# Two score tiles converted in one VectorE instruction, against single-tile conversions in two separate PSUM tiles, with a re-set planner

## The chip, the cores and the metric

The kernel runs on one core of a Trainium2 chip. The metric is the device time of one execution in microseconds (us). Five engines work side by side, each in the order in which its own instructions stand in the program: TensorE (PE in the profile: matmuls; PEld: its weight loads), VectorE (DVE), ScalarE (ACT), GpSimd (POOL) and SyncE (SP, which here issues nearly all DMAs). Engines wait for each other through semaphores.

## The reference

Two attention blocks share the input `x` (2048 rows, 512 columns, 32 heads of width 16) and are mixed by a gate:

```python
g = sigmoid((x * gate_w).sum(-1))
a = A(x): q,k,v = x @ wqkv; softmax(q k^T / 4) v over all 2048 keys; @ wo
b = B(x): the same, but each query sees 8 keys: itself and those 2,4,...,14 rows before; @ wo
out = g * a + (1 - g) * b
```

A needs 32 x 2048 x 2048 exponentials. In tiles of 128 keys by 512 queries of one head these are 2048 score tiles, called units below.

## The kernel before, in words

**Periods.** The 32 heads are 8 groups of 4, and the queries 4 blocks of 512. A pair of group and block is a period: 32 periods with 16 key tiles x 4 heads = 64 units each.

**Two ways for a unit.** Most units go through ScalarE: PE writes scores into a ring of two PSUM tiles `ring` of 3 and 2 units in turn (`fillA`), ACT computes the exponential of 3 or 2 units at once into `pT` (1536 or 1024 elements per partition), and PE multiplies with V into `acc` (`pvA`, groups of four matmuls in four column strips). Some go through VectorE, four at a time (a quad, made by `make_quad`): PE writes one unit into one of two PSUM banks named `m` (`fillD`), DVE turns the scores into an integer that read as bfloat16 approximates the exponential (`conv`, writes `dt`), DVE makes two shifted copies for a better approximation (`term`, 2048 elements per partition each), and PE adds all three, weighted, into `acc` (`pvD`, three groups of four matmuls). When a period's units are all in, DVE transposes `acc` to `accT`, takes the reciprocal `rden`, POOL scales into `ott`, DVE transposes back.

**The same two banks serve everything else on PE**: projections of K, Q, V (evacuated by DVE to `kr`, `qr`, `vp_all`), B's projections (`bw` times `xT`, evacuated to `kvs`), the sum over B's window (`ident` times `pv`), the output projections (`woarr`, `bwo`, evacuated to `osb`). In the kernel before, both banks are one tile, allocated once, and a user gets a half of it:

```python
mm_t = ps.tile([128, 2, QW], FP32, tag="mm", bufs=1, name="mm_ps")
def misc_ps(hold, shape):
    v = mm_t[:, hold.k, 0:math.prod(shape[1:])]
```

**B's local attention** runs tile by tile (16 tiles of 128 rows, `b_tile`) on POOL: products `prod`, sums `lg`, softmax with help of DVE and ACT, products `pv`, then PE sums over the window.

**The order is planned at build time.** `Sched` is a list scheduler written in Python: each operation has an engine, a planned duration, dependencies, resources (`acq`, `rel`), and a due time. Step by step it takes the operation that can start soonest, the earliest due first among near ones, and emits its instructions; this fixes the order on each engine. The waits between engines are not the planner's: the tile framework sets semaphores from the tiles that the emitted instructions read and write. The planner counts the two `m` banks as two resources.

**Names that the change touches.** `STREAM` and `LEAST` (L59, L60) steer zero-weight passes: `warm` asks what share of the last 3413 ns PE streamed and puts in passes of four matmuls with weights of zero, for free if the share is under `STREAM`, and at the cost of a delay (up to 450 ns) if it is under `LEAST`. `MARGIN` adds slack to planned hand-overs between engines. `join` (in `make_quad`) puts two units of a quad together where both banks are free at the planned time: two fills, then one `conv` over 1024 elements. `start_quad` and `d_source` decide when a quad is begun (`LATE`, `QUAD`, `UNIT`, at most 3 at once). `hooks` sets, at the begin of each period, the due times of projections and starts B's tiles (`b_next`, one for each 1.7 periods).

Of the kernel before, what the change touches and what calls it, by code (L numbers as in the profile page):

```python
# [23 lines left out]
QW = 512  # L24
# [12 lines left out]
def _mean_log_ratio():  # L37
    n = 4096
    acc = 0.0
    for k in range(n):  # L40
        y = 128.0 * k / n
        s = 0.0
        for o, w in zip(OFFS, WTS):
# [10 lines left out]
SEM = 50.0  # L54
PASS = 216.0
SWITCH = 100.0
OVERDUE = 500.0
KB_NS = 6.5
XFER = 1900.0  # L59

MARGIN = {("POOL", "DVE"): 1500.0, ("POOL", "PE"): 1500.0, ("DVE", "PE"): 200.0, ("PE", "DVE"): 60.0,
          ("ACT", "DVE"): 1000.0, ("DVE", "POOL"): 800.0, ("SP", "PE"): 1000.0, ("DVE", "SP"): 300.0, ("SP", "POOL"): 1500.0, ("POOL", "ACT"): 1000.0}
WINDOW = 3413.0
STREAM = 0.48
LEAST = 0.42
FAST = 682.0


# [7 lines left out]
class Op:  # L76
    __slots__ = ("eng", "fn", "dur", "mms", "deps", "due", "allow", "acq", "rel", "lat", "start", "fin", "vis",
                 "name", "not_before", "after", "begun", "prompt", "zeros", "closing",
                 "lock", "gap", "kb", "ahead")

    def __init__(self, eng, fn, dur=0.0, mms=None, deps=(), due=None, allow=1000.0, acq=(), rel=(), lat=0.0,
                 name="", not_before=0.0, after=None, begun=(), prompt=False,
                 lock=False, kb=0.0):
        self.ahead = None
        self.kb = kb
        self.eng, self.fn, self.dur, self.mms = eng, fn, dur, mms
        self.deps = [d for d in deps if d is not None]
        self.due, self.allow, self.acq, self.rel, self.lat = due, allow, list(acq), list(rel), lat
        self.begun = [d for d in begun if d is not None]
        self.start = self.fin = self.vis = None  # L90
        self.prompt = prompt
        self.zeros = 0
        self.closing = False
        self.lock = lock
        self.gap = 30.0
        self.name, self.not_before, self.after = name, not_before, after
# [26 lines left out]
class Sched:  # L123
# [82 lines left out]

    def commit(self, op, ready):
        e = op.eng
        if op.ahead is not None:
            op.ahead(max(ready, self.t[e]))  # L210
        for h in op.acq:
            h.k = self.slots[h.res].take()
        if e == "PE":
# [107 lines left out]
    def pick_pe(self, near, cands):  # L321
        urgent = [c for c in cands if c[0].name == "fillA"]
        first = min(max(self.t["PE"], c[1]) for c in near)
        same = [c for c in near if c[0].mms[0][0] == self.pe_mode]
        tight = [c for c in near if c[0].mms[0][0] != self.pe_mode and c[2] < first + 600.0 and c[0].name != "fillA"]
        order = (same + [c for c in near if c not in same]) if same and not tight else near
        if not urgent:
            return order[0]
        u = urgent[0]
        limit = u[2]  # L330
        for c in order:
            if c[0] is u[0]:
                return c
            _, _, st = self.pe_run(c[0].mms, c[1])
            first, _, _ = self.pe_run(u[0].mms, u[1], st)
            alone, _, _ = self.pe_run(u[0].mms, u[1])
            if first <= max(limit, alone + 30.0):
                return c
        return u
# [3 lines left out]
def kernel(  # L343
# [58 lines left out]
    def mm(out, lhsT, rhs, start, stop, **kw):  # L402
        return T.matmul(out, lhsT=lhsT, rhs=rhs, start=start, stop=stop, **kw)
# [16 lines left out]
    for k in range(KEPT, KEPT + 28):  # L420
        S_.slots["keep"].free[k] = INF


    mm_t = ps.tile([128, 2, QW], FP32, tag="mm", bufs=1, name="mm_ps")

    def misc_ps(hold, shape):
        v = mm_t[:, hold.k, 0:math.prod(shape[1:])]
        if len(shape) > 2:
            v = v.rearrange("p (a b) -> p a b", a=shape[1])
        return v  # L430

    def sb(hold, shape, dtype, name):
        return work.tile(shape, dtype, name=name, tag=f"{hold.res}_{hold.k}", bufs=1)
# [795 lines left out]
    def pe_source(e):  # L1229
# [8 lines left out]
        if us and w < INF:  # L1238
# [3 lines left out]
            if r < INF and S_.slots["pTA" if n == 3 else "pTB"].when() < INF:  # L1242
# [3 lines left out]
                op = Op("PE", None, mms=[("r", u[2], 512) for u in us], name="fillA")  # L1246
                op.fn = lambda us=us, res=res, n=n, op=op: emit_fill(us, res, n, op)
                op.after = after_fill
                outl.append((op, r, act_idle - 480.0))

        if pv_wait:
            p = pv_wait[0][0]
# [13 lines left out]
            if whole or full:  # L1266
                a = acc_ready(p)
                if a is not None:
                    vs = [vp_ops[(u[1], 4 * periods[p][1] + u[2])].vis for u in batch]
                    if all(v is not None for v in vs):  # L1270
# [5 lines left out]
                        op.closing = npv[p] <= 8  # L1276
                        op.fn = lambda p=p, batch=batch, op=op: emit_pva(p, batch, op)
                        op.after = lambda o, p=p, batch=batch: after_pva(o, p, batch)
                        outl.append((op, r, batch[0][3] + (2000.0 if sum(used) < 5 else -2000.0)))

        for q in pvd_ready:
            a = acc_ready(q["p"])
# [10 lines left out]
            op.closing = npv[q["p"]] <= 8 and q["next"] == len(OFFS) - 1  # L1293
            op.fn = lambda q=q, op=op: emit_pvd(q, op)
            op.after = lambda o, q=q: after_pvd(o, q)
            outl.append((op, r, min(q["vis"] + 4000.0, q["late"])))
            break
        return outl

# [93 lines left out]
            pv_commit(q["p"], op)  # L1393


    LATE = 2000.0
    QUAD = 6000.0
    UNIT = 470.0
    quad_at = [0]
    quad_end = [None]  # L1400
    JOIN = 100.0

    def soon(o, late):
        if o.due is not None:
# [35 lines left out]
    def make_quad(p, t, late):  # L1440
# [4 lines left out]
        def term_tile():  # L1445
            q["terms"].append(sb(hq[len(q["terms"])], [128, 4, QW], U16, "dt"))
        aops, fops = [], []
        holds, both = [Hold("m") for _ in range(4)], set()

        def fill(j):  # L1450
            f_ = fops[j]
            for _ in range(f_.zeros):
                mm_ct(mm_t[:, 0 if j in both else holds[j].k, :], zw, ones_t[:], True, True)
            for j_ in ((j, j + 1) if j in both else (j,)):
                mm(mm_t[:, j_ - j if j in both else holds[j].k, :], kt_all[32 * j_:32 * j_ + 32, i, t * 128:(t + 1) * 128],
                   qt_tiles[periods[p]][32 * j_:32 * j_ + 32, :], True, True, tile_position=(32 * j_, 0))

        def conv(j):
            if j == 0:
                term_tile()  # L1460
            V.tensor_scalar(out=q["terms"][0][:, j:j + 2, :] if j in both else q["terms"][0][:, j, :],
                            in0=mm_t[:] if j in both else mm_t[:, holds[j].k, :], scalar1=EXP_MULT, scalar2=EXP_ADD,
                            op0=ALU.mult, op1=ALU.add)

        def join(j, at):

            f1, f2, a1, a2 = fops[j], fops[j + 1], aops[j], aops[j + 1]
            if S_.slots["m"].when(2) + (MARGIN["DVE", "PE"] if at > 25000.0 else 0.0) > at + JOIN:
                return
            both.add(j)  # L1470
            S_.pend["PE"].remove(f2)
            S_.pend["DVE"].remove(a2)
            f1.mms = f1.mms + f2.mms
            f1.acq += f2.acq
            a1.rel += a2.rel
            a1.dur = 1217.0

            def same(o, o2):
                o2.start, o2.fin, o2.vis = o.start, o.fin, o.vis
            f1.after = lambda o: same(o, f2)  # L1480
            a1.after = lambda o: same(o, a2)
        for j in range(4):
            f_ = S_.add(Op("PE", lambda j=j: fill(j), mms=[("r", j, 512)], deps=[qt_ops[periods[p]][0], kdep(p, t)],
                           begun=fops[-1:] or [quad_end[0]], allow=0.0,
                           acq=[holds[j]] + ([] if j else hq[:1]), name="fillD"))
            fops.append(f_)
            quad_end[0] = f_
            a_ = S_.add(Op("DVE", lambda j=j: conv(j), dur=683.0, deps=[f_] + aops[-1:], due=min(S_.now, late - 6000.0) + 300.0 * j - 5000.0,
                           rel=[holds[j]], name="conv"))
            aops.append(a_)  # L1490
            if j % 2 == 0:
                f_.ahead = lambda at, j=j: join(j, at)
        tops = []
        for k in range(1, len(OFFS)):
            def term(k=k):
                term_tile()
                V.tensor_scalar(out=q["terms"][k][:], in0=q["terms"][0][:], scalar1=float(OFFS[k]), scalar2=None, op0=ALU.add)
            tops.append(S_.add(Op("DVE", term, dur=FAST, lock=True, deps=aops + tops[-1:], acq=[hq[k]], due=min(S_.now + 7000.0 + 1500.0 * k, late - 4000.0 + 1000.0 * k), name="term")))

        def done(o):  # L1500
            d_busy[0] -= 1
# [3 lines left out]
        d_busy[0] += 1  # L1505

    def d_source(e):
        if e == "PE" and d_busy[0] < 3:
            if any(o.due is not None and o.due < S_.now and S_.est(o) is not None for o in S_.pend["PE"] if o.name != "fillD"):
                return []  # L1510
            dve = sum(o.dur for o in S_.pend["DVE"] if S_.est(o) is not None)
            if dve + max(0.0, S_.t["DVE"] - S_.now) < 3000.0 and S_.now > 22000.0:
                start_quad()
        return []

# [22 lines left out]
    def hooks(p):  # L1538
# [7 lines left out]
            g_jobs(now + 8000.0)  # L1546
        m = p // 8
        if p % 8 == 1 and m + 1 < NPR:
            k_due(m + 1, now + 0.3 * TPER, 4.2 * TPER)
            v_due(8 * m + 8, 8 * m + 16, now + 1.5 * TPER, 4.5 * TPER)  # L1550
        if p % 2 == 0 and p + 2 < NP:
            q_pair(periods[p + 2][0], periods[p + 2][1] // 2, now + 0.8 * TPER)
        if p == NP - 8:
            wo_jobs([o for i_ in range(NG) for o in kt_ops[i_]] + list(vp_ops.values()))
        while b_proj_next[0] < NT and b_proj_next[0] <= p + 1:
            b_proj(b_proj_next[0], now + (2000.0 if p > 2 else 22000.0))
            b_proj_next[0] += 1
        if len(b_proj_ops) == NT and all(o.start is not None for o in b_proj_ops):
            b_proj_ops.clear()
            for k in range(KEPT + 16, KEPT + 28):  # L1560
                S_.slots["keep"].give(k, now)
        while b_next[0] < NT and b_next[0] * 1.7 <= p:
            b_tile(b_next[0], now + (2000.0 if p > 2 else 22000.0))
            b_next[0] += 1

# [67 lines left out]
```

## Time and profile before

| | |
|---|---|
| three runs | 963.09, 963.73, 969.73 us; median 963.73 |
| profiled execution | 963.73 us, span 961.9 us, mean granted PE clock 0.888 |
| busy | PE 800.3, ACT 765.5, DVE 640.0, POOL 608.3 us |
| ACT, exponentials | 643 instructions for 1608 units, 758.1 us busy, 154.7 us idle just before them |
| DVE, conversions | 398 of 512 elements (684 ns), 21 of 1024 (1213 ns) |
| DVE, terms | 220 of 2048 elements, 859 ns |
| zero-weight matmuls | 728 into `acc` (128 of them open its 32 periods), 20 into the `m` banks, 24 into `ring` |

The span runs from the first to the last instruction of the core; the execution is 1.8 us longer. "Idle before" counts the time an engine stood still just ahead of an instruction, and the releaser is the instruction whose end let it go. Because a helper records every operation, all instructions carry one line number, so groups are told apart by tiles: `mm_ps` is the tile of the two `m` banks. A granted clock of 1.0 is PE at full speed and 0.5 at half; the trace has it in windows of 3.41 us.

### The profile page before, as it was taken

The numbers are of one execution on the slowest core, as the hardware profiler recorded it, in microseconds if no ns is written. First come the engines' busy times: TensorE is split into PE (matmuls) and PEld (weight loads), VectorE is DVE, ScalarE is ACT, GpSimd is POOL, SyncE is SP. The second block draws the span as 40 slices with busy tenths as digits, with TensorE's granted clock in tenths as the row PEclk, the third lists the DMA queues.
The fourth block names the chain that finished last, engine by engine and source line by source line (L and its number), as shares of the span: only waits on it lengthen the run. The fifth ranks groups of instructions, "written<-read, shape, count | busy, mean of one in ns | idle before, by whom it ended". The sixth has DMA issues, their size and how long they took to land.

```text
span 961.9 us, 25343 instructions
## 1 busy us (share of the span) xinstructions
PE 800.3 (83%) x10830; PEld 252.0 (26%) x10830; DVE 640.0 (67%) x1009; ACT 765.5 (80%) x665; POOL 608.3 (63%) x909
## 2 busy tenths in 40 slices
PE   6888887988888887888879888787799998898975
PEld 2232222322232232222213223232312132222221
DVE  4646766577846777577667695778767676665644
ACT  1977778897975997789778899888878798779880
POOL 1015867788236978598187897979765789862300
PEclk9988899997987999899779989999967599779797
DMA  9121022230202123021211212122121213110000
GB/s 220 46 95 66 29 83 79 78 116 26 80 19 89 45 90 117 22 91 50 79 61 46 72 46 84 45 73 88 37 72 45 72 51 88 47 61 30 12 7 28
DMA packets 66801, 62.09 MB, mean 65 GB/s; under 512 B 14848, under 2 KB 64128, under 8 KB 66688
## 3 DMA queue, kind: packets, MB, share of 16 engines
q1 hardware_dynamic: 65104, 60.28, 19.9%
q8 instruction: 84, 1.38, 0.6%
q10 hardware_dynamic: 1584, 0.20, 0.1%
q14 instruction: 29, 0.24, 0.1%
HBM read 43.91 MB, written 12.62 MB: 59 GB/s over the span
## 4 chain that ended last, share of the span: by engine, by line
PE 54%; DVE 32%; ACT 8%; issue 4%; DMA 0%; DVEq 0%; ACTq 0%
PE mm_ps L393 29%; DVE dt L393 22%; PE acc L393 15%; PE ring L393 9%; ACT pT L393 8%; DVE kvs L393 2%; DVE qr L393 1%; DVE kr L393 1%; DVE kt_all L393 1%; DVE vp_all L393 1%; DVE osb L393 1%; DVE accT L393 1%; DVE kmax_all L393 1%; PE warm L393 1%; DVE bw L393 1%
## 5 line engine op out<-in xcount | busy, mean ns | idle before, releaser
L393 ACT ACTIVATE pT<-ring 128x1536 bf16<-128x1536 f32 (+1 forms) x643 | 758.1, 1249 | 154.7 <-PE ring L393 132.5
L393 DVE TENSOR_SCALAR dt<-mm_ps 128x512 uint16<-128x512 f32 (+1 forms) x419 | 292.7, 710 | 178.4 <-PE mm_ps L393 135.3
L393 PE MATMUL ring<-qt,kt_all 32*128 32x512 bf16 x1608 | 306.6, 419 | 11.9 <-ACT pT L393 9.8
L393 PE MATMUL mm_ps<-qt,kt_all 32*128 32x512 bf16 x440 | 159.3, 424 | 78.7 <-DVE dt L393 57.7
L393 POOL TENSOR_TENSOR pv<-vsh,lg 128x256 bf16<-128x256 bf16 x256 | 175.0, 706 | 32.6 <-PE mm_ps L393 17.7
L393 POOL TENSOR_TENSOR prod<-ksh,qb 128x256 f32<-128x256 bf16 x256 | 180.9, 736 | 16.4 <-DMA ksh<-kv_scr 12.6
L393 DVE TENSOR_SCALAR dt<-dt 128x2048 uint16<-128x2048 uint16 x220 | 186.2, 859 | 1.9 <-PE acc L393 0.3
L393 POOL TENSOR_TENSOR prod<-prod 128x256 f32<-128x256 f32 (+1 forms) x256 | 183.6, 727 | 5.6
L393 PEld LDWEIGHTS <-kt_all 32*128 32x128 bf16 (+1 forms) x2304 | 88.2, 93 | 348.5 <-issue 335.1
L393 PE MATMUL acc<-pT,vp_all 128*17 128x512 bf16 x1608 | 143.3, 425 | 0.0
L393 POOL TENSOR_TENSOR ott<-accT,rden 128x256 bf16<-128x256 f32 x31 | 22.3, 721 | 139.8 <-DVE rden L393 139.8
L393 PE MATMUL acc<-dt,vd_all 128*17 128x512 bf16 x880 | 83.3, 416 | 0.0
L393 PE MATMUL acc<-ones_t,zw 128*32 128x512 bf16 x728 | 76.7, 473 | 3.1 <-DVE accT L393 2.6
L393 PE MATMUL mm_ps<-bw,xT 128*32 128x512 bf16 x768 | 61.8, 416 | 17.2 <-DVE dt L393 11.7
L393 PEld LDWEIGHTS <-vp_all 128*17 128x17 bf16 x2048 | 41.3, 91 | 95.1 <-issue 83.8
L393 POOL TENSOR_TENSOR lg<-lg,rr 128x256 f32<-128x256 f32 x16 | 10.7, 669 | 75.7 <-DVE rr L393 67.7
L393 PEld LDWEIGHTS <-xT 128*32 128x32 bf16 (+1 forms) x1920 | 38.4, 101 | 63.4 <-issue 57.3
L393 PE MATMUL acc<-dt,vp_all 128*17 128x512 bf16 x440 | 48.4, 429 | 0.0
L393 PE MATMUL mm_ps<-ident,pv 128*32 128x128 bf16 x2048 | 40.7, 222 | 6.4 <-DVE dt L393 5.6
L393 DVE CAST kvs<-mm_ps 128x512 bf16<-128x512 f32 x32 | 21.7, 683 | 25.8 <-PE mm_ps L393 21.9
L393 PEld LDWEIGHTS <-pv 128*32 128x32 bf16 x2048 | 32.3, 97 | 22.0 <-issue 18.3
L393 PEld LDWEIGHTS <-zw 128*32 128x32 bf16 x772 | 19.2, 102 | 70.6 <-issue 67.0
(82 smaller groups left out, 409.4 us busy)
## 6 DMA issues: line engine op xcount, KB each, us to landing
ksh<-kv_scr SPq DMA_DIRECT2D x16, 1024.0 KB
vsh<-kv_scr SPq DMA_DIRECT2D x16, 1024.0 KB
kv_scr<-kvs SPq DMA_DIRECT2D x16, 384.0 KB
q_scr<-qr SPq DMA_DIRECT2D x32, 128.0 KB
qt<-q_scr SPq DMA_DIRECT2D x31, 128.0 KB
qb<-kv_scr SPq DMA_DIRECT2D x16, 128.0 KB
out_dram<-osb SPq DMA_DIRECT2D x16, 128.0 KB
kt_all<-kr SPq DMA_DIRECT2D x112, 16.0 KB
```

What stands on the lines that cost most here:

```text
L393: return chain_on(key, f(*a, **k))
```

## The change

The conversion is always of one unit: `join` goes away, and with it the one tile over two banks. Each bank is a tile of its own (`m0_ps`, `m1_ps`), allocated anew for each user. Beside this, planner constants and due times are set anew. GpSimd's halved instructions and the zero-weight passes that may delay PE are in both kernels; of the passes only the two thresholds change.

```diff
-OVERDUE = 500.0
+OVERDUE = -500.0
-MARGIN = {("POOL", "DVE"): 1500.0, ...
+MARGIN = {("POOL", "DVE"): 1000.0, ...
-STREAM = 0.48
-LEAST = 0.42
+STREAM = 0.56
+LEAST = 0.40
...
-        tight = [c for c in near if ... and c[2] < first + 600.0 and ...]
+        tight = [c for c in near if ... and c[2] < first + 1300.0 and ...]
...
-    mm_t = ps.tile([128, 2, QW], FP32, tag="mm", bufs=1, name="mm_ps")
-
-    def misc_ps(hold, shape):
-        v = mm_t[:, hold.k, 0:math.prod(shape[1:])]
-        if len(shape) > 2:
-            v = v.rearrange("p (a b) -> p a b", a=shape[1])
-        return v
+    def misc_ps(hold, shape, dtype=FP32):
+        return ps.tile(shape, dtype, tag=f"m{hold.k}", bufs=1, name=f"m{hold.k}_ps")
...
-                outl.append((op, r, act_idle - 480.0))             # due of fillA
+                outl.append((op, r, act_idle - 580.0))
-    ... batch[0][3] + (2000.0 if sum(used) < 5 else -2000.0)        # due of pvA
+    ... batch[0][3] + (2750.0 if sum(used) < 5 else -2000.0)
-    ... min(q["vis"] + 4000.0, q["late"])                           # due of pvD
+    ... min(q["vis"] + 2000.0, q["late"])
-    LATE = 2000.0
-    QUAD = 6000.0
-    UNIT = 470.0
+    LATE = 750.0
+    QUAD = 7250.0
+    UNIT = 450.0
...
-        def join(j, at):
-            f1, f2, a1, a2 = fops[j], fops[j + 1], aops[j], aops[j + 1]
-            if S_.slots["m"].when(2) + (MARGIN["DVE", "PE"] if at > 25000.0 else 0.0) > at + JOIN:
-                return
-            both.add(j)
-            ...
-            a1.dur = 1217.0
         for j in range(4):
...
-                           begun=fops[-1:] or [quad_end[0]], allow=0.0, ...
+                           begun=fops[-1:] or [quad_end[0]], allow=250.0, ...
-            # due of conv: ... + 300.0 * j - 5000.0;  of term: S_.now + 7000.0 + 1500.0 * k
+            # due of conv: ... + 300.0 * j - 5500.0;  of term: S_.now + 6000.0 + 1500.0 * k
...
-        if e == "PE" and d_busy[0] < 3:
-            if any(... o.due < S_.now and ...
+        if e == "PE" and d_busy[0] < 2:
+            if any(... o.due < S_.now - 4000.0 and ...
-            if dve + ... < 3000.0
+            if dve + ... < 3250.0
...
-            k_due(m + 1, now + 0.3 * TPER, 4.2 * TPER)
+            k_due(m + 1, now + 0.60 * TPER, 5.00 * TPER)
-            q_pair(..., now + 0.8 * TPER)
+            q_pair(..., now + 0.65 * TPER)
-        while b_proj_next[0] < NT and b_proj_next[0] <= p + 1:
+        while b_proj_next[0] < NT and b_proj_next[0] * 1.05 <= p + 1:
-        while b_next[0] < NT and b_next[0] * 1.7 <= p:
+        while b_next[0] < NT and b_next[0] * 1.60 <= p:
```

## The prediction

> **What bounds the kernel now.** I read the page first, then the waits, then the timeline where the waits are longest.
>
> ```profile
> PE 800.3 (83%) x10830; PEld 252.0 (26%) x10830; DVE 640.0 (67%) x1009; ACT 765.5 (80%) x665; POOL 608.3 (63%) x909
> ...
> PE 54%; DVE 32%; ACT 8%; issue 4%; DMA 0%; DVEq 0%; ACTq 0%
> ...
> L393 ACT ACTIVATE pT<-ring 128x1536 bf16<-128x1536 f32 (+1 forms) x643 | 758.1, 1249 | 154.7 <-PE ring L393 132.5
> ```
>
> ACT's exponentials cannot be spared: 758.1 us for 1608 units, 0.4715 us a unit. They run from 23.6 us of the span to 940.1, and in these 916.5 us ACT stands still for 158.3 (counted between exponentials; the page's 154.7 is close). So the time is a floor of about 805 us (23.6 before, 758.1, 21.8 behind, 1.8 around the span) plus ACT's idle time, which nearly always ends with a `ring` fill by PE. The chain that ended last is hardly ACT: it goes to and fro between PE and DVE. The waits say where:
>
> ```profile
> DVE dt L393 <- PE mm_ps L393: 135.3, 144, 4.0
> ACT pT L393 <- PE ring L393: 132.5, 186, 4.1
> PE mm_ps L393 <- DVE dt L393: 94.1, 164, 1.6
> ...
> PE mm_ps L393 <- DVE kvs L393: 12.9, 22, 1.2
> ```
>
> PE, in order, waits for DVE to read an `m` bank, and what stands behind it is the next ring fill. One stretch of the timeline shows what kind of wait this is:
>
> ```profile
> 917.23 0.63 PE L393 MATMUL mm_ps<-ident,pv 128*32 128x128 bf16 x32
> ...
> 917.69 0.61 PE L393 MATMUL mm_ps<-bwo,bw 128*32 128x512 bf16 x8
> ...
> 918.35 0.69 DVE L393 CAST kt_all<-mm_ps 128x512 bf16<-128x512 f32 x1 [1.41 <-PE mm_ps L393]
> ...
> 919.09 0.61 PE L393 MATMUL mm_ps<-bwo,bw 128*32 128x512 bf16 x8 [0.47 <-DVE kt_all L393]
> ```
>
> The `ident,pv` matmuls fill bank 0 and end at 917.86. The `bwo,bw` matmuls fill bank 1. DVE's cast reads bank 0, yet starts at 918.35, 0.05 us after the first eight `bwo,bw` end at 918.30; the second eight, into bank 1, start 0.05 us after the cast of bank 0 ends. Each waits for work in the other bank: the banks are halves of one tile, and the program's waits are set for the tile.
>
> I followed the semaphore values of the program before through its order. Of 400 matmuls into the banks that wait for DVE, 319 wait for something later than the last reader of their own bank; of 556 DVE reads, 249 wait for a write later than the last one into theirs. Matched with the trace's starts (start, less the later of 0.22 us after the previous matmul and 0.05 us after the own bank was read), these waits hold PE for 157 us in all, 310 of them noticeable at 0.51 us on average; DVE loses 109 us in the same way, 183 times 0.59. Waits for the own bank cost PE 4.5 us.
>
> **The change, part by part.**
>
> *Two tiles instead of one.* The same walk through the program after finds one matmul waiting for a reader of the other bank, and no DVE read waiting for a later write. So the 157 us of PE waits lose their cause. How much reaches the end? For each exponential I set ACT's idle time before it against the other-bank waits on PE since the previous ring fill, and take the smaller: 81 us in all. With one fill further back it is 109 us, since a ring fill that was late makes the next late. I take 81, because the waits for ACT, mode switches and own banks that stand beside them remain (PE also waits 46 us for ACT, and 54 us pass at changes between row and column tiling). Next late after these is PE's own stream, then ACT.
>
> *Conversions of one unit.* 21 wide ones at 1213 ns go; a pair costs 2 x 684 = 1368, so 155 ns more each, 3.3 us of DVE. But there are fewer quads: 105 for 110. Conversions on DVE go from 398 x 0.684 + 21 x 1.213 = 297.7 us to 420 x 0.684 = 287.3, terms from 220 to 210, 8.6 us less. DVE is freed of 19 us, at 67% busy and off the path in itself: 0 us. If DVE's slack were gone, 3.3 us would be the price of the narrow form.
>
> *Twenty more units on ACT.* The 5 quads return as 20 units: 20 x 0.4715 = +9.4 us (10.7 at the 0.537 us a unit that full-clock windows of this trace take with their idle time). On PE 20 fills move from `m` to `ring`, 60 matmuls of terms go and 20 with `pT` come: 10 groups of four fewer, 2 us at 0.22 each (eight matmuls in 0.61 us against four in 0.39), off ACT's path.
>
> *Zero-weight passes.* 856 matmuls instead of 772, 21 more groups of four, 4.6 us of PE. 24 into `ring`, ahead of a delayed fill, become none; so the added ones stand where the plan has room: 0, at worst +4.6. Their gain in clock is bounded below.
>
> *The end.* Before, the last exponential ends at 940.1, but two quads are unfinished, and `accT` of the last period starts at 951.42: 11.4 us later. In the new order no conversion follows the last ring fill: there come the last window sum, eight matmuls with `pT` (0.6 us), and the transpose. From the transpose to the end (10.5 us) the work is the same. I take -10; bounds -11 and, if the window sum is late, 0.
>
> *Order and dues.* B's projections start 5% further apart (last one from unit 915 to 981 of 2048), the last window sum moves from unit 1987 to 2038, K projections by 0 to 80 units. Past SP's queue the same DMAs go in another order; the last K projections stand at units 427, 945 and 1477, ahead of the head groups that begin at 512, 1024 and 1536 by 59 units or more, some 26 us at 916.5/2048 = 0.45 us a unit of either kind, against stores and loads that the page shows with DMA at 20%. 0 us, unless POOL paces (below).
>
> *The clock.* 64 windows of 3.41 us run at half clock, in 29 stretches. Units take 0.537 us in full-clock windows and 0.774 in half: a half-clock window loses 3.41 x (1 - 0.537/0.774) = 1.05 us, 67 us for all, part of it the idle time already counted. Every full-clock window in which PE streamed under 0.36 of its capacity (fills counted as a quarter of the array) was followed by half clock, none above 0.37 was. PE's work for a unit stays the same, and with fewer waits each window holds more: I take 0 beyond the 81, bounds -8 (eight windows) and +10. The Trainium skill ("TensorE: Matmul & The Clock Gate", Terms) prices the throttled time as that time x (1 - K/N): an estimate of 109 us for these 218 us. The trace's 67 decides; by the page's price the eight windows would give -14 instead of -8.
>
> The skill's "PSUM — Partial Sum Buffer" (Summary) advises to let a reader use another bank while a matmul runs; the row above shows the program doing the opposite. If the other bank were no refuge after all, the sum would lack its 81.
>
> **The sum**, against the profiled execution, which is also the median: 963.7 - 81 + 9.4 - 10 + 0 = **882 us**, 8.5% less.
>
> **The rivals.**
>
> *The waits come back on the own bank.* DVE is in order, and a quad's fills are planned to follow conversions closely (0.2 us of margin); a DVE instruction held up by POOL (terms take 859 ns against planned 682) delays the bank. For it: 173 of the 319 other-bank waits, and 82 of their 157 us, stand before a quad's fill, where a conversion is never far. Against it: own-bank waits cost 4.5 us now, and DVE's own 109 us go too. Half of the 81 lost: 963.7 - 40.5 + 9.4 - 5 = 928.
>
> *POOL paces the end.* Tile 5 of B is through on POOL at 431.4 us and tile 15 at 897.2: 46.6 us a tile. The new order has the last window sum 10 units before the end. If POOL keeps this pace whatever the others do: 897 + 10 x 0.537 + 13 (the last `pT` matmuls, some 2 us for what follows the window sum, and the 10.5 from the transpose on) = 916. Against it: POOL is busy 38 us of a tile's 46.6; it waits 139.8 us (51.9 of them at the start) for `rden` and 103 for DVE's part of the softmax, both of which come earlier when DVE and PE do.
>
> *The waits removed were free.* If PE's time is not what held ACT: 963.7 + 9.4 - 10 = 963, no change. Against it: 132.5 us of ACT's idle time end with a ring fill.
>
> *Slower: the clock falls.* Passes that may delay PE are put in under 0.40 instead of 0.42, near the 0.37 of the trace, and none is left in front of a ring fill. If more windows fall to half clock, each costs 1.05 us. From 882 it takes 87 further ones to reach 973 and be slower by 1%; that is 151 of 279 windows instead of 64. Time 975. Against it: 21 more passes, and fewer waits.
>
> **How the numbers follow.** Forecast 0.66, own-bank waits 0.13, POOL 0.10, no change 0.06, slower 0.05. A difference of 1% is about what a measurement of this kernel can tell from none. The first three are faster by over 1%: 0.89; same 0.06; slower 0.05. The forecast's own range is 845 (109 instead of 81, -11 at the end, -8 for the clock: 963.7 - 109 + 9.4 - 11 - 8) to 905 (58 instead of 81, if only the waits ahead of a bank's first matmul count: 963.7 - 58 + 9.4 - 10). The range given goes to 940, where a third of the 81 and 6 us at the end are left (963.7 - 27 + 9.4 - 6): it takes in the first two rivals.
>
> **What would show it.** In the profile after: the sum of PE's waits for DVE at the banks well under half of its 94.1 and 12.9 us; ACT's idle time before exponentials near 75 us instead of 154.7, with 651 instructions and 768 us busy; the last exponential some 12 us before the end instead of 22; a mean clock of 0.89 or above; ACT with a larger part of the chain. Wrong would be: banks' waits gone but ACT's idle time over 120 us (PE was not the holder), PE waiting for `pv` of POOL, or a clock under 0.85.

## The result and the profile after

The kernel after takes 828.25 us (median of four runs, 821.29 to 839.06), the one before beside it 966.4. The ratio is 0.8546, with a 95% interval of 0.8475 to 0.8618. Times here and below are medians of all runs; a run over 1.5% above the fastest of its kernel counts as slow (of these four, 839.06), and the ratios are of the fast runs alone. The forecast was 882 with a range of 845 to 940: the way was right, but the time lies below the range, and the gain of 138 us (134 between the two profiled spans) was forecast as 82. The profiled execution took 829.57 us, its span is 827.7.

The same lines of the page, after:

```profile
PE 758.0 (92%) x10874; PEld 248.6 (30%) x10874; DVE 628.6 (76%) x1000; ACT 754.9 (91%) x673; POOL 618.2 (75%) x909
...
PEclk9798998999999969999999977998999999999899
...
POOL 41%; PE 21%; ACT 16%; DVE 13%; issue 6%; SPq 2%; DMA 1%; POOLq 0%; DVEq 0%; ACTq 0%
...
L390 ACT ACTIVATE pT<-ring 128x1536 bf16<-128x1536 f32 (+1 forms) x651 | 746.6, 1306 | 43.9 <-PE ring L390 42.1
```

ACT is busy for 91% of the span, with 43.9 us of idle time before exponentials instead of 154.7. PE fell from 54% of the chain that ended last to 21% and DVE from 32% to 13%; POOL leads it with 41%, from nothing. The waits say who waited for whom (us in total, times, longest):

```profile
DVE dt L390 <- PE m_ps L390: 53.7, 58, 4.0
ACT pT L390 <- PE ring L390: 42.1, 61, 1.9
...
PE m_ps L390 <- DVE dt L390: 20.7, 31, 2.2
...
PE m_ps L390 <- DVE kvs L390: 1.3, 2, 1.1
```

PE's waits for conversions fell from 94.1 us in 164 places to 20.7 in 31. The timeline after shows that a reader and a writer of different banks now run side by side:

```profile
820.57 0.71 DVE L390 TENSOR_SCALAR kt_all<-m_ps,gate 128x512 f32<-128x512 f32 x1
820.70 0.40 PE L390 MATMUL m_ps<-woarr,oat 128*32 128x512 bf16 x4 [0.87 <-DVE oat L390]
```

DVE reads one bank from 820.57 to 821.28, and PE's matmuls into the other begin at 820.70. The bracket says what they had waited for: their own operand `oat`, not the reader of the other bank.

By the first and the last exponential the two traces split the 134 us without a rest (us of the span):

| | before | after | difference |
|---|---|---|---|
| start of the first exponential | 23.6 | 18.8 | -4.8 |
| exponentials, net of overlap | 758.1 | 746.6 | -11.5 |
| ACT's idle time between them | 158.3 | 52.4 | -105.9 |
| from the last exponential to the end | 21.9 | 9.8 | -12.1 |

### The profile page after: what moved, and what is told of

It reads as the page before. It is cut to its first block, busy times and chain, and to the rows that moved or that the text cites. A ratio compares the mean times of both kernels' runs of the same rounds, so it can differ in the third digit from the quotient of the medians.

```text
span 827.7 us, 25428 instructions
## 1 busy us (share of the span) xinstructions
PE 758.0 (92%) x10874; PEld 248.6 (30%) x10874; DVE 628.6 (76%) x1000; ACT 754.9 (91%) x673; POOL 618.2 (75%) x909
## 4 chain that ended last, share of the span: by engine, by line
POOL 41%; PE 21%; ACT 16%; DVE 13%; issue 6%; SPq 2%; DMA 1%; POOLq 0%; DVEq 0%; ACTq 0%
POOL prod L390 27%; ACT pT L390 16%; PE m_ps L390 10%; POOL pv L390 9%; DVE dt L390 8%; PE acc L390 6%; PE ring L390 5%; POOL lg L390 3%; SPq L390 2%; POOL ott L390 1%; DMA wkv<-in_A_wqkv_dram 1%; DVE rr L390 1%; POOL kt_all L390 1%; DVE qr L390 0%; DVE kmax_all L390 0%
## 5 line engine op out<-in xcount | busy, mean ns | idle before, releaser
L390 ACT ACTIVATE pT<-ring 128x1536 bf16<-128x1536 f32 (+1 forms) x651 | 746.6, 1306 | 43.9 <-PE ring L390 42.1
L390 DVE TENSOR_SCALAR dt<-m_ps 128x512 uint16<-128x512 f32 x420 | 278.6, 679 | 89.0 <-PE m_ps L390 53.7
L390 PE MATMUL ring<-qt,kt_all 32*128 32x512 bf16 x1628 | 285.2, 395 | 33.1 <-ACT pT L390 28.0
L390 PEld LDWEIGHTS <-kt_all 32*128 32x128 bf16 (+1 forms) x2304 | 98.1, 92 | 324.1 <-issue 310.8
L390 PE MATMUL m_ps<-qt,kt_all 32*128 32x512 bf16 x420 | 154.6, 395 | 19.4 <-DVE dt L390 15.0
L390 PE MATMUL acc<-pT,vp_all 128*17 128x512 bf16 x1628 | 133.1, 395 | 0.0
L390 PE MATMUL acc<-dt,vd_all 128*17 128x512 bf16 x840 | 73.0, 390 | 0.2 <-DVE dt L390 0.2
L390 PE MATMUL m_ps<-bw,xT 128*32 128x512 bf16 x768 | 57.4, 393 | 5.2 <-DVE dt L390 4.1
L390 PE MATMUL m_ps<-ident,pv 128*32 128x128 bf16 x2048 | 42.3, 228 | 0.4 <-DVE dt L390 0.4
L390 DVE CAST kvs<-m_ps 128x512 bf16<-128x512 f32 x32 | 21.8, 682 | 13.5 <-PE m_ps L390 13.5
L390 POOL TENSOR_TENSOR lg<-lg,rr 128x256 f32<-128x256 f32 x16 | 11.3, 707 | 26.1 <-DVE rr L390 23.7
```

The lines of the kernel that those rows point to most:

```text
L390: return chain_on(key, f(*a, **k))
```

## The experiments

Theory A is the prediction's: the one tile over two banks makes PE and DVE wait for the other bank, and that is what held ACT. Theory B: the new dues and thresholds brought the gain. Theory C: the wide conversions did the harm, since they need both banks at once. Ratios are to the kernel before on the same chip, with a 95% interval; runs stood on several chips, so where a time and a ratio disagree the text gives both.

**One tile or two, old dues or new (e1, e2, e3).** e1 switches joining off in the kernel before; e2 has the same instruction order, and a tile for each bank. e3 is the kernel after, with one tile again.

```diff
 e1
-    JOIN = 100.0
+    JOIN = -1.0e9
 e2 (besides, the fill and the conversion of one unit written as in the kernel after)
-    mm_t = ps.tile([128, 2, QW], FP32, tag="mm", bufs=1, name="mm_ps")
-    def misc_ps(hold, shape):
-        v = mm_t[:, hold.k, 0:math.prod(shape[1:])]
...
+    def misc_ps(hold, shape):
+        return ps.tile(shape, FP32, tag=f"m{hold.k}", bufs=1, name=f"m{hold.k}_ps")
 e3: the same lines the other way round, in the kernel after
```

> The kernel before with joining switched off; the one tile over two banks and all old constants stay. Theory A (waits for the other bank, made by the one tile): the waits stay, so no large change, 945 to 985 us. Theory B (the new dues and thresholds brought the gain): the same, 945 to 985. Theory C (the wide conversions themselves cost the time, since a pair needs both banks free at once): most of the gain is here, 830 to 880.

> The same program order as e1, instruction for instruction; only each bank is a tile of its own. Old constants. Theory A: nearly the whole gain, 825 to 870 us, with PE's waits for DVE at the banks down from over 90 us to under 30 and ACT's idle time before exponentials under 75. Theory B: at most a fifth of the gain, 930 to 970. Theory C: as e1.

> The kernel after, same order instruction for instruction, but with both banks again in one tile (no joining). Theory A: the gain is lost, 940 to 985 us, ACT idle 130 us or more before exponentials. Theory B: the gain stays, 830 to 860. Theory C: the gain stays, 830 to 860.

| | one tile | two tiles |
|---|---|---|
| old dues, joined | 968 (before) | not tried |
| old dues, no joining | e1: 957.29, 0.9874 (0.9767 to 0.9981) | e2: 820.36, 0.8502 (0.8423 to 0.8581) |
| new dues, no joining | e3: 958.75, 0.9859 (0.9807 to 0.9911) | after: 828.25, 0.8546 (0.8475 to 0.8618) |

From one tile to two it is 137 us with the old dues and 131 with the new; from old dues to new it is under 2 us with one tile and 8 with two (1 in e10 and e11 below). Theories B and C fall. Joining gave nothing that shows: without it the one-tile kernel is 0.2 to 2.3% faster, with two quads more. The waits of e1, then e2's line of ACT and its chief wait on PE:

```profile
ACT pT L393 <- PE ring L393: 147.9, 198, 3.6
...
PE mm_ps L393 <- DVE dt L393: 104.5, 179, 2.2
```

```profile
L393 ACT ACTIVATE pT<-ring 128x1536 bf16<-128x1536 f32 (+1 forms) x640 | 732.3, 1306 | 34.9 <-PE ring L393 33.7 <-PE m_ps L393 0.5
```

```profile
PE m_ps L393 <- DVE dt L393: 16.6, 29, 2.0
```

**The clock (e4, e5).** Is the carrier the wait itself, or the fall of PE's clock that it brings about? Half-clock windows fell from 64 to 24 between the two kernels. e4 is the kernel after without zero-weight passes, e5 is e1 with far more of them. With other passes the planner also makes a somewhat different plan.

```diff
 e4
-    S_.filler = zero_pass
+    S_.filler = None
 e5
-STREAM = 0.48
-LEAST = 0.42
+STREAM = 0.75
+LEAST = 0.55
```

> The kernel after without any zero-weight pass (the planner's filler is off; the opening of acc stays). It prices the clock: in the profile after a half-clock window costs 3.41 x (1 - 0.470/0.813) = 1.44 us, and 24 are left. Theory A says the clock rose because the waits went, so the passes matter little more than before: 10 to 40 further half-clock windows, 840 to 885 us. Theory B, in which the new thresholds keep the clock up: 60 or more further windows, over 910.

> As e1 (one tile, old dues, no joining), but thresholds 0.75 and 0.55 instead of 0.48 and 0.42: 1644 zero-weight matmuls instead of about 800, which should keep PE's clock up while the waits for the other bank stay. It separates two carriers of the 134 us. Theory A1 (the waits hold PE directly; the clock is a small part): half-clock windows fall from 56 to under 25, and the time only to 915 to 950 us. Theory A2 (the waits cost mainly because they drop the clock): with the clock up the time comes to 840 to 890 us although the waits are there.

e4 took 861.09 us (0.8908, 0.8839 to 0.8976), with 69 half-clock windows, 45 more than the kernel after. Without the passes it is 33 us slower, but 11 of these lie behind the last exponential (20.6 us instead of 9.8): in e4's plan conversions are still to come there. e5 took 941.71 (0.9810, 0.9749 to 0.9872), with 29 windows instead of e1's 56 (mean clock 0.948). So with the waits in place a nearly restored clock returns 16 us of 137 by the times and 6 by the ratios, whose intervals overlap, passes and their own time together. That is far from the 840 to 890 us of A2. A1 is right: most of what the waits cost they cost directly. The price of a window is not settled: e4's 33 us for 45 windows make 0.7 us at most, 0.5 without the end, and e5's 6 to 16 for 27 make 0.2 to 0.6. All are well under the 1.05 and 1.44 that the unit rates gave. A likely reason, not shown, is that units are also slow in these windows because something else is late there.

**Which waits (e13, e14, e15).** The prediction priced PE's waits and gave DVE's nothing. These three are e2 with the waits put back by hand: PE's alone, DVE's alone, both.

```diff
+    def other_bank(key, bi, a, k):          # called for each instruction; this is e15
+        if key == "pe":
+            w = bank_of(a[0]) if a else None
+            if w is not None:
+                if True and read_of[1 - w] is not None:          # False in e14
+                    tc.add_manual_dep(bi.ins, read_of[1 - w].ins.name, hold_info, ...)
+                write_of[w] = bi
+        elif key in ("dve", "act"):
...
+                    if True and key == "dve" and write_of[1 - r] is not None:          # False in e13
+                        tc.add_manual_dep(bi.ins, write_of[1 - r].ins.name, hold_info, ...)
+                    read_of[r] = bi
```

> As e2 (two tiles, old dues, same order), but PE's matmuls into a bank are made to wait for DVE's last read of the other bank, as in e1: 345 of 411 such waits. DVE does not wait in turn. The prediction built its 81 us on PE's waits alone. If that was the right carrier: 890 to 910 us (e2 and some 81 us). If DVE's waits, priced at nothing, carry as much: 850 to 880.

> As e2, but DVE's reads of a bank are made to wait for PE's last write into the other one, as in e1: 273 of 585 reads. PE does not wait in turn. If DVE's waits are covered by its slack (it is at 80%): 820 to 835 us. If they carry a share of their own: 845 to 890.

> As e2 with both kinds of waits put back by hand, so that the wait counts equal e1's; each bank is still a tile of its own. If the waits are all that the one tile does: e1's 950 to 965 us. If the one tile costs something else, less.

e13: 858.77 us (0.8902, 0.8839 to 0.8966), 38 more than e2. e14: 826.19 (0.8551, 0.8479 to 0.8622), 6 more. e15: 956.13 (0.9838, 0.9771 to 0.9905), 136 more (by the ratios 39, 5 and 129). e15 can't be told from e1: within this noise the waits are all that the one tile does. Together the two kinds cost three times their sum.

Part of this the traces show. In e13 PE has the same 345 waits for the other bank as in e1, but they hold it 112 us instead of 167, 0.34 us each instead of 0.50. DVE's reads lose 66 us in e14 and 111 in e1, where PE waits as well. So the waits themselves grow, from 178 us apart to 278 together. The account that fits is that a conversion that waits for the other bank's write ends later, the next write waits for that conversion, and so on: each lateness is handed back. But the same waits also cost the end less while there is slack: in e14 66 us of DVE's waits cost 6. POOL has 35% of the chain that ended last in e2, nothing in e13 and 2% in e1, which suggests that POOL's pace covered the first of PE's waits. And the clock moves as well: 20 half-clock windows in e2, 31 in e13, 56 in e1. How much of the jump each of the three makes up, no run tells.

```profile
ACT pT L415 <- PE ring L415: 72.0, 100, 3.3
...
PE m_ps L415 <- DVE dt L415: 52.1, 112, 1.7
```

These are e13's waits; e1 has 147.9 and 104.5 in the same rows, e2 33.7 and 16.6. In e13 and e15 the wait put back stands at the weight load ahead of the matmul, in e1 at the matmul; the row of PE is all but the same in e15 (101.2) as in e1.

**POOL (e8, e12).** POOL leads the chain after. e8 issues one product in four of B's scores twice on POOL in the kernel after; e12 does the same in e1.

```diff
-                G.tensor_tensor(out=st["prod"][...], ...)
+                for _ in range(2 if w_ % 2 and lo else 1):
+                    G.tensor_tensor(out=st["prod"][...], ...)
```

> The kernel after, with one product in four of B's scores issued twice on POOL (the planner does not know): 64 more instructions of 0.75 us, 48 us more on POOL, the same output and the same order of all else. If POOL paces the kernel after (41% of its chain that ended last): 860 to 880 us. If POOL has slack (window sums start 2.6 to 58 us after POOL is through; 93 us waiting for rden, 50 of them at the start): 828 to 845.

> As e1 (one tile, old dues, no joining), with the same 64 additional instructions on POOL as in e8, some 45 us of POOL's time. With the waits in place POOL waited 156 us for rden, so it should have had slack: 955 to 970 us, under a third of its additional work. If POOL paced the kernel already then: 990 to 1005.

e8: 867.13 us (0.9033, 0.8989 to 0.9076), 39 more by the times and 47 by the ratios, for 40 us more of POOL's busy time (658.3 against 618.2). e12: 962.82 (1.0049, 1.0006 to 1.0092), 5.5 us over e1 by the times and 17 by the ratios, for 50 us more (660.2 against 610.6). With one tile POOL had slack for most of it; without the waits its added work lengthens the kernel about one for one. It is no wait of PE for `pv`: window sums of the kernel after start 2.6 us or more after POOL is through with a tile. A way that its waits show leads through DVE, which stands in order before `mx` until POOL's sums are there: 15.0 us in the kernel after, 42.9 in e8. No run tried this way by itself.

```profile
DVE mx L390 <- POOL lg L390: 42.9, 14, 5.0
```

```profile
POOL 59%; PE 16%; ACT 10%; DVE 8%; issue 5%; SPq 1%; DMA 1%; POOLq 0%; DVEq 0%; ACTq 0%
```

These are e8's wait and its chain by engine.

**Attempts to go further (e6, e7, e9), and the dues again (e10, e11).** e6 is e2 with thresholds 0.65 and 0.47. e7 is the kernel after with the old rules for admitting quads. e9 is e2 with `ott` scaled on DVE in all periods:

```diff
 e9
-            (V if last else G).tensor_tensor(...)
+            V.tensor_tensor(...)
-               Op("DVE" if last else "POOL", scale, dur=450.0 if last else 616.0, due=-1.0, ...)
+               Op("DVE", scale, dur=450.0, **(dict(due=-1.0) if last else dict(allow=a)), ...)
```

> As e2 (two tiles, old dues), with thresholds 0.65 and 0.47: 1232 zero-weight matmuls. e2 has 20 half-clock windows left; at 1.44 us each they would be worth 29 us, by e4 (45 windows more, 33 us more) 0.73 us each, 15 us. If the clock still costs: 800 to 812 us with under 10 such windows. If the passes now delay PE more than they save: 825 to 840. Beats both kernels if it works.

> The kernel after with the old constants that admit quads (LATE, QUAD, UNIT, 3 at once, the two tests in d_source): 110 quads instead of 105, so 20 units fewer on ACT. Theory: a unit costs ACT 0.4586 us where it runs nearly without idle time, so 20 x 0.4586 = 9 us less: 815 to 824 us, with the exponentials' busy time near 737. If POOL paces: no change, 826 to 832.

> As e2 (two tiles, old dues), with the scaling of accT into ott on DVE in all periods, not only in the last: 31 instructions of 0.72 us leave POOL (22 us), 31 of 0.43 us come to DVE (13 us), and DVE no longer waits for POOL before it transposes back. e8 gave 39 us more for 40 us more work on POOL. If POOL paces e2 too: 798 to 812 us. If DVE, now at 80%, is the tighter one: 820 to 835.

> The same program as e2, timed again beside e11, to tell the dues apart. If the new dues cost time: 817 to 824 us here and 826 to 832 in e11. If they make no difference: the two within 4 us of each other.

> The kernel after, timed again beside e10. If the new dues cost time: 826 to 832 us, 5 to 12 above e10. If they make no difference: within 4 us of e10.

e6: 831.73 us (0.8658, 0.8578 to 0.8739), with 17 half-clock windows, hardly fewer than e2's 20, and more idle time on ACT (61 us against 49): the passes bring nothing. That they delay is likely (11 us by the times, 7 to 15 by the ratios of e10 and e2), but its plan is different too, with 645 exponentials instead of 640. e7: 841.81 (0.8763, 0.8681 to 0.8844), a miss: the exponentials' net time did fall, to 736.6, but ACT's idle time rose to 73.0 and the end to 15.5. Why old admission fits badly with the other new constants stays open. e9: 818.92 (0.8562, 0.8513 to 0.8611), e10: 821.01 (0.8591, 0.8535 to 0.8647), e11: 822.04 (0.8593, 0.8551 to 0.8636): not to be told apart. So the new dues neither gain nor cost anything that shows, and neither does taking the scaling off POOL; that its relief and DVE's burden cancel is a guess. No version here is clearly faster than the kernel after.

## Why the prediction was right in its cause and wrong in its sizes

**Right: the cause.** The row of waits, the stretch of timeline and the wait values named the false waits, those for the other bank. e2 against e1 and e15 against e2 show that they make the difference between the columns.

**Failed: DVE's waits at no price, and with them the term -81, measured -106.** The step was to set ACT's idle time against PE's waits since the previous ring fill, to take the lower of two values (81 and, with one fill further back, 109), and to let DVE's 109 us go for nothing. e13 to e15 show that this is not how the time is made up: PE's waits alone cost 38 us, well under 81, and DVE's alone 6, but DVE's on top of PE's cost 97 (91 by the ratios). So the other value, 109, came near the measured 106 without the reason being right. How far the loop, slack and the clock make up the missing 25 stays open. The clock was bounded at eight windows and gained 40; at e4's 0.5 us a window that alone would be 20.

**Failed: +9.4 for twenty more units, measured -11.5 on the same row.** The price of 0.4715 us a unit was net time divided by units and held fixed. But an exponential that follows at once starts before the one ahead of it ends. Start to start they are 1.331 us (three units) and 0.904 (two) apart, while a lone one takes 1.451 and 1.024: 0.12 us less. Before, 368 of 643 followed at once, after 556 of 651: 188 x 0.12 = 22.6 us, which with the 9.4 gives -13. So each wait that went took an overlap's worth with it. The Trainium skill has this rule ("ScalarE: Activation LUTs", What ACT_TABLE_LOAD costs, which says that back-to-back activations overlap by about 93 ns); the trace has 120, and the rule would have told to split the row. This term had no range of its own. It is what carried the time out of the range: the low end of 845 already took 109, -11 and -8, and with -11.5 in place of +9.4 it would be 824.

**Nearly right: the end, -10 forecast, -12.1 measured.** No conversion follows the last ring fill, as read from the order. e3, with the new order and one tile, needs 11.3 us from its last exponential to the end, so most of the 12 is the order's and little the waits'. **Missing: the start, -4.8.** The same banks serve the first projections, which the sum left out. Exponentials begin at 23.6 to 24.3 us in the one-tile kernels and at 18.8 to 20.8 in those with two. e15 begins at 20.2 although it has both kinds of waits: they were put back for reads by DVE, not for those by ACT. ACT's first read of a bank starts at 12.34 us in e1, at 10.96 in e15 and at 10.53 in e2. What makes up the rest of the 4 us no run tried by itself.

**Half right: the clock.** Half-clock windows went from 64 to 24 as waits went; the way was right, the bound of eight windows was not. **Right: the conversions.** The 3.3 us for narrow conversions were nowhere to be seen.

**The rivals.** The waits came back on the own bank in small part only. Counted from 0.22 us after the previous matmul to 0.05 us after the own bank was read, such waits hold PE 39 us after, in 89 places; before it is 18, where the prediction has 4.5. POOL did not keep its 46.6 us a tile: tile 5 is through at 370.4 and tile 15 at 799.8, 42.9 a tile, so the 916 fell. But its suspicion was sound at another time: e8 shows that work added to POOL counts once the waits are gone, at 828. POOL is not the pace alone: e9 has 17 us less of its busy time than e2 (607.0 against 624.1) and gains nothing that shows. The prediction named PE's own stream and then ACT as what would be late next, and had POOL only as a rival. The clock did not fall: 0.951 against 0.888.

## What to carry to other kernels

Where a scheduler written by hand counts two buffers as two resources, look whether the framework that sets the waits counts them so: two banks in one tile are one thing to it, and its waits can be read from the semaphore values without any chip. Two engines that each wait needlessly for the other can cost much more than the two kinds of wait apart (here 136 us against 38 and 6), so price them together, and ask what slack hides one kind alone. And a price per unit read from a row with idle time in it changes when the idle time goes.

## What the runs showed of the hardware

PE's clock followed its streaming with a sharp edge. Count 0.216 us for 512 columns, the commonest distance of a matmul from the fourth before it at full clock, and a quarter of it for each matmul on 32 rows or 32 columns, since four of them run side by side. Then in the trace before the fullest of the 29 full-clock windows that were followed by half clock had 0.366 of its 3.41 us streamed, and the emptiest that was followed by full clock 0.371. In the trace after the two are 0.352 and 0.372. At half clock, where the same columns take twice the time, windows followed by full clock had 0.745 or more before and 0.759 or more after; those followed by half clock had up to 0.742 (one 0.767) and 0.734. Raising the thresholds for zero-weight passes in e6 did not pay, though 20 such windows were left in e2.
